# A fixed order for the first four chunks of a gated recurrence, with filler products, and two PSUM banks swapped in the last half

## The chip, the cores and the metric

The kernel runs on one core of a Trainium2 chip. A core has five engines with queues of their own: TensorE (PE, matmuls, with its weight loads as PEld), VectorE (DVE), ScalarE (ACT), GpSimd (POOL) and SyncE (SP, which here issues nearly all transfers). The metric is device time of the whole program in microseconds. The kernel before took 556.48 us, the median of three runs (555.96 to 556.78).

## The reference

Two blocks stand one behind the other. The first is a gated recurrence over 4 batches, 8 heads, 768 positions and a head dimension of 48:

```python
for t in range(S):
    state = alpha[:, :, t, :, None] * state + np.einsum('bhd,bhe->bhde', k[:, :, t], v[:, :, t])
    y[:, :, t] = np.einsum('bhd,bhde->bhe', q[:, :, t], state)
```

Its result, with the heads side by side, is x with 3072 rows and 384 columns. The second block is `h = x @ w_in` (384 x 2048), `g = h * sigmoid(h)`, and `g @ w_out` (2048 x 384). The weights come as 64-bit floats and are turned into 32-bit ones on the chip.

## The kernel before

The recurrence is worked in 24 chunks: 128 positions of one batch, all eight heads in four pairs. Chunk n belongs to batch n mod 4. The first eight chunks take the path that this change touches.

For one chunk, `products(n)` (L710) transposes alpha, k and q on TensorE, four 128x128 transposes each. ScalarE copies the transposed alpha to SBUF (L731). VectorE runs a scan backwards over it (L734), takes the smallest products (L737), multiplies k (L745, tile `kp`), and then, in `quotient`, takes a reciprocal (L762), scans forwards (L764) and multiplies q (L770, tile `p`). `scores(n)` multiplies kp by qp on TensorE, 16 small matmuls into two PSUM tiles; ScalarE copies each to `g` (L812) and GpSimd sets what lies in the future to zero (L813); then kp is transposed and copied to `kn` (L832). `values(n)` multiplies v by g into x (`xt`, copied at L863), and `states(n)` makes the new state from kn and v (L882).

The dense layer is a list of pieces, each 12 or more matmuls long, that `go_on` runs one at a time. The first 16 are `enter_plain` (from L911): 12 matmuls of 128x256 from xt and w_in into one of three PSUM banks, then a Silu on ScalarE (L923). The first needs the x of chunks 0 and 1 and the first three converted pieces of w_in; pieces three and four need six, and so on to twelve. The conversion of one piece is in `weights` (from L614): a transfer of 512 KB of 64-bit words (`bits`, four buffers, issued by SP at L519 in `fetch`), a rounding copy on ScalarE (L629, tile `up`) and three VectorE instructions (L645 to L647). The next rounding copy and the next transfer are issued within the conversion.

The main loop goes over steps. Step s runs scores of chunk s - 1, products of chunk s, values and states of chunk s - 1, and after each of its four slots `fill` (L1184) gives conversions and dense pieces by a due time: up to slot 10 the first three conversions, later pieces, with conversions before each. Through the first steps a planner in the compiler then orders the instructions of each engine by its own costs, and may move any that is not pinned. `keep_in_program_order` pins an instruction behind the one traced before it on its engine. TensorE is pinned only late (`late`, from the end of step 7 at the earliest); in these steps only the rounding copies and the first VectorE instruction of each conversion are.

PSUM has eight banks: three for the recurrence (`ps_a`), three for dense pieces in (`ps_m`), two for dense pieces out (`ps_o`). In the first chunks the transposed k and q use `ps_o` or `ps_m` banks. `leave` (L1035) multiplies g by w_out for half a group: seven pieces, with two accumulators `a` and `b` from `new(i)`, which takes output bank i. The last product of a half is in bank 0, and the half after it starts in bank 0 too. Between halves other work usually lies; at the very end two halves of the last group follow each other directly.

Of the kernel before, what the change touches and what calls it, by code (L numbers as in the profile page):

```python
# [355 lines left out]
def quotients(  # L356
# [23 lines left out]

    def in_order(ins):

        return tc.keep_in_program_order(ins) if late else ins

    class pe:
        @staticmethod
# [49 lines left out]
        return ps_a.tile([128, 512], F32, name="ps_a").rearrange("p (j c) -> p j c", c=n)  # L436


    table = fix.tile([128, 1], F32, name="table")
    dve.memset(table, 0.0)  # L440
    act.activation(table, table, AF.Silu)
    ident = consts.tile([128, 128], F32, name="ident")
    make_identity(nc, ident)

# [21 lines left out]
    def load(n, names="akq"):  # L466
        if n == NT:
            return
        c = ctxs.setdefault(n, dict(zip(("ci", "b"), divmod(n, B))))
        b, rows = c["b"], slice(c["ci"] * C, c["ci"] * C + C)  # L470
        for name, src in (("a", alpha), ("k", k), ("q", q)):
            if name not in names:
                continue
            x = src[b, :, rows, :]
            if n < NA:
                c[name] = nat[name][n % NIN]
                nc.sync.dma_start(c[name][:, :, 0:D], x.transpose([1, 0, 2]))
                continue

            c[name] = late["quads"][name]
            for u in range(2):
                for i in range(2):
                    r = 64 * u + 32 * i
                    nc.sync.dma_start(
                        c[name][r : r + 32, 32 * (1 - i) :][:, 0 : 4 * NP * D].rearrange(
                            "p (g c) -> p g c", g=NP),
                        x[u::2].rearrange("h (b j) d -> b h (j d)", j=4))

    NV = 2
# [4 lines left out]
    def load_v(n):  # L496
        c = ctxs.setdefault(n, dict(zip(("ci", "b"), divmod(n, B))))
        x = v[c["b"], :, c["ci"] * C : c["ci"] * C + C, :].transpose([1, 0, 2])
        t = c["v"] = vns[n % NV]
        if n < NA:  # L500
            nc.sync.dma_start(t[:, :, 0:D], x)
            return
        nc.sync.dma_start(t[:, 0 : H // 2, 0:D], x[:, 0 : H // 2])
        for e in range(2):
            nc.sync.dma_start(t[CH * e : CH * e + CH, H // 2 :, 0:D], x[CH - CH * e : C - CH * e, H // 2 :])
# [7 lines left out]
    def fetch():  # L513

        if wide and sources:
            src = sources.pop(0)
            n = src.shape[1]
            bits = raw.tile([128, 512, 2], I32, name="bits")[:, 0:n, :]
            nc.sync.dma_start(bits.rearrange("p n w -> p (n w)"), src.bitcast(I32))  # L519
            coming.append(bits)  # L520

    load(0)
# [91 lines left out]
    def weights(which):  # L614

        pieces = [
            (w_in[:, t, c : c + 512], moe_w_in[t * 128 : t * 128 + 128, c : c + 512])  # L620
            for t, c in pieces_in
        ] if which == 0 else [
            (w_out[:, f, :], moe_w_out[f * 128 : f * 128 + 128, :]) for f in range(NFT)]
        def rounding(bits):
            n = bits.shape[1]
            up = upp.tile([128, 512], I32, name="up")[:, 0:n]

            tc.keep_in_program_order(
                act.activation(up, bits.bitcast(U32)[:, :, 0], AF.Copy, scale=2.0**-29))  # L629
            return up  # L630

        ahead = []
        for i, (dst, src) in enumerate(pieces):
            if not wide:
                act.dma_start(dst, src)
                yield
                continue
            assert which == 0 or conv_done[0] == n_conv[0]
            bits = coming.pop(0)
            up = ahead.pop() if ahead else rounding(bits)  # L640
            if which == i == 0:
                yield
            hi, w = bits[:, :, 1], dst.bitcast(I32)
            tc.keep_in_program_order(
                dve.tensor_scalar(w, hi, 3, 0x3FFFFFFF, ALU.logical_shift_left, ALU.bitwise_and))  # L645
            dve.scalar_tensor_tensor(w, hi, -(1 << 30), w, ALU.bitwise_and, ALU.bitwise_or)
            dve.tensor_tensor(w, w, up, ALU.add)  # L647
            if i + 1 < len(pieces):
                ahead.append(rounding(coming[0]))
            fetch()  # L650
            yield
# [55 lines left out]
        x = x[:, 32:].rearrange("p (g j d) -> p g j d", j=4, d=D)  # L707
        dve.transpose(to.rearrange("p g (b j) -> p g j b", j=4), x[:, :, :, 0:32])

    def products(n):  # L710

        c = ctxs[n]
        sg = seg[0 if late else n % 2]
        ps = {}

        for name in ("a", "k", "q"):
            if n >= NA:
                if name == "a":
                    turned(c[name], tokens(sg))
                    load(n + 1, "a")  # L720
                continue
            if n < GB and name != "a":

                at = "kq".index(name)
                ps[name] = (bank(at) if n == 1 else out_bank(at, 512)).rearrange("p (j c) -> p j c", c=C)
            else:
                ps[name] = ps_attn()
            for j in range(NP):
                pe.transpose(ps[name][:, j, :], c[name][:, 2 * j : 2 * j + 2, :], ident)
            if name == "a":  # L730
                act.copy(tokens(sg), ps[name])  # L731
        end = NP * W
        u = upool.tile([128, end + 1], F32, name="u")
        dve.tensor_tensor_scan(u[:, end - 1 :: -1], sg[:, end:0:-1], one[:, end:0:-1],  # L734
                               0.0, ALU.mult, ALU.add)

        dve.tensor_single_scalar(least[:, n, :], u[:, 0:end:W], 2.0**-64, ALU.max)  # L737
        kp = c["kp"] = turns(kps, n) if n < NA else kps[0]
        ut = tokens(u)
        if n >= NA:  # L740
# [1 line left out]
            turned(c["k"], ps["k"])  # L742
            load(n + 1, "k")
        if n < NA:
            dve.tensor_tensor(kp, ps["k"], ut, ALU.mult)  # L745
            quotient(n, sg, ps["q"])
            return
        j = NP // 2
# [5 lines left out]
    def quotient(n, sg=None, q=None):  # L754
# [4 lines left out]
                return  # L759
            sg = c.pop("sg")  # L760
        end, iv = NP * W, inv
        dve.reciprocal(iv[:, 0:end:W], least[:, n, :])  # L762
        p = turns(qps if n < NA else [qps[0], late["p"]], n)
        dve.tensor_tensor_scan(p[:, 0:end], sg[:, 0:end], iv[:, 0:end], 0.0, ALU.mult, ALU.add)  # L764
# [5 lines left out]
        dve.tensor_tensor(qp, q, qp, ALU.mult)  # L770

    def flip(n):

# [18 lines left out]
    def scores(n):  # L792
# [6 lines left out]
        for j in (0, 2, 1, 3):  # L799
            for e in range(2 if n >= NA else 1):  # L800
                for u in range(2):
# [5 lines left out]
        g = decayed.rearrange("p (u j c) -> p u j c", u=2, j=NP)  # L807
        swapped = decayed.rearrange("p (o u j c) -> p o u j c", o=2, u=2, j=NP // 2)
        c["g"] = (lambda u, j: g[:, u, j, :]) if n < NA else (
            lambda u, j: swapped[:, j // 2, u, j % 2, :])  # L810
        for u in range(2 if n < NA else 0):
            act.copy(g[:, u], ps[u])  # L812
# [14 lines left out]
        if n < NA and ci < NCH - 1:  # L827
            ps_k = ps_attn()
            for j in range(NP):
                pe.transpose(ps_k[:, j, :], c["kp"][:, j, :], ident)  # L830
            c["kn"] = work.tile([128, NP, C], F32, name="kn")
            act.copy(c["kn"], ps_k)  # L832
        if ci > 0:
            s = st[b].rearrange("p j u e -> p j (u e)")
            for j in range(NP):
# [3 lines left out]

    def values(n):

# [18 lines left out]
        act.copy(xts[half][:, :, e * C : (e + 1) * C], py[:, 0:NKT])  # L863
    def states(n):
        c = ctxs.pop(n)
        ci, b, vn = c["ci"], c["b"], c["v"]
        if ci < NCH - 1:
# [8 lines left out]
            for u in range(2):  # L876
                r = slice(64 * u, 64 * u + D)
                s, x = st[b][r, :, u, :], ps[r, :, 0:D]
                if ci > 0:
                    dve.tensor_tensor(s, x, s, ALU.add)  # L880
                else:
                    act.copy(s, x)  # L882

    def block_x(grp, at):

# [25 lines left out]
    def enter_plain(grp, h, pair):  # L911
# [4 lines left out]
        for f in range(8 * pair, 8 * pair + 8, 2):  # L916
# [6 lines left out]
            act.activation(gts[grp, h, pair][:, i : i + 2, q % 2, :], ps, AF.Silu)  # L923
# [111 lines left out]
    def leave(grp, h):  # L1035
# [30 lines left out]
                sums_w(2 * grp + h - 1, 4 * next(steps) + 4)  # L1066

        def new(i):
            return out_bank(i, HO)

        a, b = new(0), new(1)
        product(a, 0, 0, b11, True)
# [111 lines left out]
    def fill(step, slot):  # L1184

        at = step * SLOTS + slot
        if at < marks[0]:
            if at == SLOTS:
                next(conv[0])
            elif step >= 1:  # L1190
                convert(0, (at - SLOTS) * 3 // (marks[0] - SLOTS) + 1)
            return
        i = next(i for i, m in enumerate(marks[1:]) if at < m)
        a, b = [work_at[n] for n in ([0] + phases)[i : i + 2]]
        due = a + (b - a) * (at - marks[i] + 1) / (marks[i + 1] - marks[i])
# [4 lines left out]
            convert(1, 3 * (done - 6) // 2)  # L1200
            go_on()

    for step in range(STEPS):
        if step == 1:
            load(NIN)
        stages = [[(scores, 1)], [(products, 0)], [(values, 1)], [(states, 1)]]
        if step == 1:

            stages = stages[1::-1] + stages[2:]
        elif 5 <= step < NA:  # L1210
# [105 lines left out]
```

## Time and profile before

| what | us |
| --- | --- |
| median of three runs | 556.48 |
| profiled execution | 557.21 |
| its span, first to last instruction | 555.4 |
| TensorE busy | 540.8 (97%) |
| VectorE busy | 446.1 (80%) |
| ScalarE busy | 208.5 (38%) |
| first transfer of alpha landed, first transpose | 4.1, 4.2 |
| first dense piece starts | 24.23 |
| last matmul ends | 550.4 |

A busy TensorE isn't TensorE at its peak: matmuls overlap, and a slow clock counts as busy. What tells more is the spacing of the starts of successive matmuls. For the 128x256 matmuls of the dense layer it is 216 ns, for the 128x192 ones 163 ns, for a transpose 213 ns at the start of the program and 109 ns later.

### The profile page before, as it was taken

The numbers are of one execution on the slowest core, as the hardware profiler recorded it, in microseconds if no ns is written. First come the engines' busy times: TensorE is split into PE (matmuls) and PEld (weight loads), VectorE is DVE, ScalarE is ACT, GpSimd is POOL, SyncE is SP. The second block draws the span as 40 slices with busy tenths as digits, with TensorE's granted clock in tenths as the row PEclk, the third lists the DMA queues.
The fourth block names the chain that finished last, engine by engine and source line by source line (L and its number), as shares of the span: only waits on it lengthen the run. The fifth ranks groups of instructions, "written<-read, shape, count | busy, mean of one in ns | idle before, by whom it ended". The sixth has DMA issues, their size and how long they took to land. (4 is left out here: it accounts for less than half of the span.)

```text
span 555.4 us, 12641 instructions
## 1 busy us (share of the span) xinstructions
PE 540.8 (97%) x5026; PEld 490.1 (88%) x5026; DVE 446.1 (80%) x801; ACT 208.5 (38%) x466; POOL 76.8 (14%) x146
## 2 busy tenths in 40 slices
PE   6999999999999999999999999999999999999996
PEld 4788887998899899899999999988998999999996
DVE  5897888983999899997998986998884796945431
ACT  2556644223333243353253353343263341332100
POOL 3110100222211212021011021021121000001000
PEclk9999999999999999999999999999999999999999
DMA  9999861254454524345445654707642135500000
GB/s 217 248 252 207 235 192 24 63 157 109 117 144 128 149 70 131 99 125 167 137 109 142 186 142 114 198 22 181 175 133 90 54 90 174 170 9 24 10 27 26
DMA packets 99217, 70.09 MB, mean 126 GB/s; under 512 B 56272, under 2 KB 88656, under 8 KB 99152
## 3 DMA queue, kind: packets, MB, share of 16 engines
q1 hardware_dynamic: 97232, 65.30, 45.0%
q0 software_dynamic: 1920, 3.93, 2.0%
q8 instruction: 40, 0.66, 0.5%
q14 instruction: 25, 0.20, 0.1%
HBM read 61.34 MB, written 7.86 MB: 125 GB/s over the span
## 5 line engine op out<-in xcount | busy, mean ns | idle before, releaser
L388 PE MATMUL ps_o<-w_out,g 128*128 128x192 f32 x768 | 133.8, 328 | 0.7 <-DVE o L1056 0.7
L388 PEld LDWEIGHTS ps_o<-w_out,g 128*128 128x128 f32 x768 | 125.7, 190 | 3.5 <-DVE o L1056 1.2
L388 PE MATMUL ps_m<-xt,w_in 128*128 128x256 f32 x480 | 113.2, 382 | 1.5 <-ACT xt L863 1.1
L388 PEld LDWEIGHTS ps_m<-xt,w_in 128*128 128x128 f32 x480 | 89.2, 190 | 14.4 <-ACT xt L863 1.6
L388 PE MATMUL ps_o<-wt,g 128*128 128x192 f32 x576 | 99.7, 326 | 0.0
L388 PEld LDWEIGHTS ps_o<-wt,g 128*128 128x128 f32 x576 | 95.1, 190 | 1.5
L388 PE MATMUL ps_m<-xc,w_in 128*128 128x256 f32 x288 | 70.7, 382 | 0.0
L388 PEld LDWEIGHTS ps_m<-xc,w_in 128*128 128x128 f32 x288 | 53.7, 190 | 6.9 <-DVE g L958 0.2
L955 ACT ACTIVATE g<-g 128x1024 f32<-128x1024 f32 x32 | 33.1, 1056 | 61.3 <-DVE g L958 61.2
L1047 DVE TENSOR_TENSOR g<-g 128x512 f32<-128x512 f32 x72 | 49.9, 706 | 7.6 <-PE ps_o L388 7.6
L825 POOL TENSOR_SCALAR_AFFINE_SELECT g<-g 64x256 f32<-64x256 f32 x64 | 34.9, 546 | 124.1 <-ACT g L818 105.4
L1059 POOL DMA_DIRECT2D out_dram<-o x40 | 22.0, 551 | 216.3 <-DVE o L1056 111.1
L388 PE MATMUL ps_m<-xc,wx 128*128 128x256 f32 x192 | 50.1, 383 | 1.0 <-DVE xc L586 1.0
L950 ACT COPY g<-ps_m 128x512 f32<-128x512 f32 x64 | 36.5, 588 | 37.1 <-PE ps_m L388 36.9
L388 PEld LDWEIGHTS ps_m<-xc,wx 128*128 128x128 f32 x192 | 35.2, 190 | 5.2 <-ACT u L1078 1.2
L958 DVE TENSOR_TENSOR g<-ps_m,g 128x512 f32<-128x512 f32 x56 | 37.1, 683 | 3.2 <-PE ps_m L388 2.7
L734 DVE TENSOR_TENSOR_SCAN u<-al,one 128x516 f32<-128x516 f32 x24 | 30.1, 1254 | 11.8 <-ACT al L731 11.5
L923 ACT ACTIVATE g<-ps_m 128x512 f32<-128x512 f32 x32 | 19.1, 597 | 40.7 <-PE ps_m L388 40.4
L950 ACT COPY part<-ps_m 128x512 f32<-128x512 f32 x32 | 18.9, 590 | 38.1 <-PE ps_m L388 24.0
L697 DVE TENSOR_REDUCE seen<-bits 128x1 f32<-128x512 int32 (+1 forms) x33 | 26.3, 821 | 6.1 <-DMA bits<-in_moe_w_in_dram 6.1
L764 DVE TENSOR_TENSOR_SCAN p<-al,inv 128x516 f32<-128x516 f32 x24 | 29.9, 1247 | 1.0 <-PE ps_a L388 0.4
L388 PE MATMUL ps_a<-g,vn 128*32 128x128 f32 x768 | 28.0, 282 | 0.5 <-POOL g L813 0.3
(129 smaller groups left out, 630.2 us busy)
## 6 DMA issues: line engine op xcount, KB each, us to landing
bits<-in_moe_w_in_dram SPq DMA_DIRECT2D x24, 512.0 KB, 4.7
bits<-in_moe_w_out_dram SPq DMA_DIRECT2D x16, 384.0 KB, 3.7
at<-in_alpha_dram SPq DMA_DIRECT2D x64, 96.0 KB, 2.6
kt<-in_k_dram SPq DMA_DIRECT2D x64, 96.0 KB, 2.6
qt<-in_q_dram SPq DMA_DIRECT2D x64, 96.0 KB, 2.6
bits<-in_alpha_dram SPq DMA_DIRECT2D x9, 512.0 KB, 4.1
out_dram<-o POOLq DMA_DIRECT2D x40, 96.0 KB, 2.3
flips<-turn SPq DMA_DIRECT2D x12, 256.0 KB, 2.4
```

What stands on the lines that cost most here:

```text
L388: in_order(nc.tensor.matmul(*args, **kw))
L697: dve.tensor_reduce(seen[kind][which][:, i : i + 1], x, axis=AX, op=op, apply_absolute_value=True))
L734: dve.tensor_tensor_scan(u[:, end - 1 :: -1], sg[:, end:0:-1], one[:, end:0:-1], 0.0, ALU.mult, ALU.add)
L764: dve.tensor_tensor_scan(p[:, 0:end], sg[:, 0:end], iv[:, 0:end], 0.0, ALU.mult, ALU.add)
L825: gps.affine_select(x, x, pattern=[[0, NP], [1, CH]], compare_op=ALU.is_ge, fill=0.0, base=0, channel_multiplier=-1)
L923: act.activation(gts[grp, h, pair][:, i : i + 2, q % 2, :], ps, AF.Silu)
L950: act.copy(to, ps)
L955: act.activation(x, x, AF.Silu)
L958: dve.tensor_tensor(to, a, b, op)
L1047: dve.tensor_tensor(cells(grp, h, pair, *to), cells(grp, h, pair, *x), cells(grp, h, pair, *y), ALU.subtract)
L1059: (gps if grp < NG - 1 else nc.sync).dma_start(out[r : r + C, c * HO : (c + 1) * HO], o)
```

## The change

A function `start` replaces the first four steps of the loop. It calls the stages of chunks 0 to 2, the products of chunk 3, all twelve conversions of w_in and seven dense pieces one by one, and while it runs (`stated[0]`) every TensorE instruction is pinned to the order in which it is called, and so are the transfers, the copies on ScalarE and the VectorE instructions that the diff wraps in `settled`. The loop goes on at step 4, without these pins, and the branch of `fill` for the first ten slots is gone. To make the order possible, `products` is split so that its transposes (`bring`) can be called alone, and `scores` so that the transposes of kp (`back`) can come later. Chunk 1 has its own g and kn in a tile `room` from the dense layer's g buffers, so that its scores needn't wait for the values of chunk 0.

`idle(n)` multiplies the identity by itself n times into a PSUM bank that nobody reads. It is called six times ahead of everything, in pairs ahead of five of the first six groups of transposes, and eight times between the kp transposes of chunk 0 and the scores of chunk 1.

In `leave`, the second half of the last group takes the two output banks the other way round.

```diff
     def in_order(ins):
-        return tc.keep_in_program_order(ins) if late else ins
+        return tc.keep_in_program_order(ins) if late or stated[0] else ins
+    stated = [True]
+    def settled(ins):
+        return tc.keep_in_program_order(ins) if stated[0] else ins
...
+    spin = banks[2].tile([128, 512], F32, name="ps_m")
+    def idle(n):
+        for _ in range(n):
+            pe.matmul(spin[:, 0:C], lhsT=ident, rhs=ident, start=True, stop=True)
...
     make_identity(nc, ident)
+    idle(6)
...
+            if n == 0 or n == 1 and name != "q":
+                idle(2)
             for j in range(NP):
                 pe.transpose(ps[name][:, j, :], c[name][:, 2 * j : 2 * j + 2, :], ident)
...
+        if n == 1:
+            room = gpool.tile([128, 4, 2, TB], F32, name="g").rearrange("p a b n -> p (a b n)")
+            c["room"] = room[:, 2 * NP * C :]
+        g = (room[:, 0 : 2 * NP * C] if n == 1 else decayed).rearrange(
+            "p (u j c) -> p u j c", u=2, j=NP)
...
+        if n != 1:
+            back(n)
...
         def new(i):
-            return out_bank(i, HO)
+            return out_bank(i ^ 1 if grp == NG - 1 and h == 1 else i, HO)
...
+    def start():
+        nonlocal bridged
+        w = lambda upto: convert(0, upto)
+        products(0)
+        products(1)
+        load(NIN)
+        next(conv[0])
+        scores(0)
+        w(1)
+        idle(8)
+        scores(1)
+        values(0)
+        back(1)
+        w(2)
+        states(0)
+        values(1)
+        bridged = 2
+        load_v(NV)
+        w(3)
+        states(1)
+        load_v(NV + 1)
+        w(4)
+        bring(2, "a")
+        w(5)
+        go_on()
+        bring(2, "kq")
+        w(6)
+        load(NIN + 1)
+        products(2)
+        go_on()
+        w(7)
+        go_on()
+        scores(2)
+        w(8)
+        go_on()
+        w(9)
+        values(2)
+        states(2)
+        load_v(2 + NV)
+        load(NIN + 2)
+        w(10)
+        bring(3, "a")
+        w(11)
+        bring(3, "kq")
+        go_on()
+        w(12)
+        products(3)
+        load(NIN + 3)
+        go_on()
+        go_on()
+        stated.pop()
+        stated.append(False)
+    start()
+    for step in range(4, STEPS):
```

More of the change, by code (lines that the diff above doesn't have):

```diff
@@ L476, in load @@
                 c[name] = nat[name][n % NIN]
-                nc.sync.dma_start(c[name][:, :, 0:D], x.transpose([1, 0, 2]))
+                settled(nc.sync.dma_start(c[name][:, :, 0:D], x.transpose([1, 0, 2])))
                 continue
@@ L500, in load_v @@
         if n < NA:
-            nc.sync.dma_start(t[:, :, 0:D], x)
+            settled(nc.sync.dma_start(t[:, :, 0:D], x))
             return
@@ L518, in fetch @@
             bits = raw.tile([128, 512, 2], I32, name="bits")[:, 0:n, :]
-            nc.sync.dma_start(bits.rearrange("p n w -> p (n w)"), src.bitcast(I32))
+            settled(nc.sync.dma_start(bits.rearrange("p n w -> p (n w)"), src.bitcast(I32)))
             coming.append(bits)
@@ L645, in weights @@
                 dve.tensor_scalar(w, hi, 3, 0x3FFFFFFF, ALU.logical_shift_left, ALU.bitwise_and))
-            dve.scalar_tensor_tensor(w, hi, -(1 << 30), w, ALU.bitwise_and, ALU.bitwise_or)
-            dve.tensor_tensor(w, w, up, ALU.add)
+            settled(
+                dve.scalar_tensor_tensor(w, hi, -(1 << 30), w, ALU.bitwise_and, ALU.bitwise_or))
+            settled(dve.tensor_tensor(w, w, up, ALU.add))
             if i + 1 < len(pieces):
@@ L708, in turned, with bring @@
         dve.transpose(to.rearrange("p g (b j) -> p g j b", j=4), x[:, :, :, 0:32])
-    def products(n):
+    def bring(n, names="akq"):
         c = ctxs[n]
         sg = seg[0 if late else n % 2]
-        ps = {}
-        for name in ("a", "k", "q"):
+        ps = c.setdefault("ps", {})
+        for name in names:
             if n >= NA:
@@ L730, in products @@
             if name == "a":
-                act.copy(tokens(sg), ps[name])
+                settled(act.copy(tokens(sg), ps[name]))
+    def products(n):
+        if "ps" not in ctxs[n]:
+            bring(n)
+        c = ctxs[n]
+        sg = seg[0 if late else n % 2]
+        ps = c.pop("ps")
         end = NP * W
         u = upool.tile([128, end + 1], F32, name="u")
-        dve.tensor_tensor_scan(u[:, end - 1 :: -1], sg[:, end:0:-1], one[:, end:0:-1],
-                               0.0, ALU.mult, ALU.add)
-        dve.tensor_single_scalar(least[:, n, :], u[:, 0:end:W], 2.0**-64, ALU.max)
+        settled(dve.tensor_tensor_scan(u[:, end - 1 :: -1], sg[:, end:0:-1], one[:, end:0:-1],
+                                       0.0, ALU.mult, ALU.add))
+        settled(dve.tensor_single_scalar(least[:, n, :], u[:, 0:end:W], 2.0**-64, ALU.max))
         kp = c["kp"] = turns(kps, n) if n < NA else kps[0]
@@ L744, in products @@
         if n < NA:
-            dve.tensor_tensor(kp, ps["k"], ut, ALU.mult)
+            settled(dve.tensor_tensor(kp, ps["k"], ut, ALU.mult))
             quotient(n, sg, ps["q"])
@@ L761, in quotient @@
         end, iv = NP * W, inv
-        dve.reciprocal(iv[:, 0:end:W], least[:, n, :])
+        settled(dve.reciprocal(iv[:, 0:end:W], least[:, n, :]))
         p = turns(qps if n < NA else [qps[0], late["p"]], n)
-        dve.tensor_tensor_scan(p[:, 0:end], sg[:, 0:end], iv[:, 0:end], 0.0, ALU.mult, ALU.add)
+        settled(dve.tensor_tensor_scan(
+            p[:, 0:end], sg[:, 0:end], iv[:, 0:end], 0.0, ALU.mult, ALU.add))
         qp = c["qp"] = tokens(p)
@@ L769, in quotient @@
             load(n + 1, "q")
-        dve.tensor_tensor(qp, q, qp, ALU.mult)
+        settled(dve.tensor_tensor(qp, q, qp, ALU.mult))
     def flip(n):
@@ L806, in scores @@
                               start=True, stop=True)
-        g = decayed.rearrange("p (u j c) -> p u j c", u=2, j=NP)
+        if n == 1:
[3 more added lines that the diff above has]
+            "p (u j c) -> p u j c", u=2, j=NP)
         swapped = decayed.rearrange("p (o u j c) -> p o u j c", o=2, u=2, j=NP // 2)
@@ L811, in scores @@
         for u in range(2 if n < NA else 0):
-            act.copy(g[:, u], ps[u])
+            settled(act.copy(g[:, u], ps[u]))
             gps.affine_select(g[:, u], g[:, u], pattern=[[0, NP], [1, C]], compare_op=ALU.is_ge,
@@ L826, in scores @@
                                       compare_op=ALU.is_ge, fill=0.0, base=0, channel_multiplier=-1)
[L827 to L832, printed above, removed]
+        if n != 1:
+            back(n)
         if ci > 0:
@@ L838, in scores, with back @@
                     tc.keep_in_program_order(mul)
+    def back(n):
+        c = ctxs[n]
+        if n >= NA or c["ci"] == NCH - 1:
+            return
+        ps_k = ps_attn()
+        for j in range(NP):
+            pe.transpose(ps_k[:, j, :], c["kp"][:, j, :], ident)
+        c["kn"] = c.pop("room")[:, 0 : NP * C].rearrange("p (j c) -> p j c", j=NP) if (
+            "room" in c) else work.tile([128, NP, C], F32, name="kn")
+        settled(act.copy(c["kn"], ps_k))
     def values(n):
@@ L862, in values @@
             xts[half] = xtp.tile([128, NKT, TB], F32, name="xt")
-        act.copy(xts[half][:, :, e * C : (e + 1) * C], py[:, 0:NKT])
+        settled(act.copy(xts[half][:, :, e * C : (e + 1) * C], py[:, 0:NKT]))
     def states(n):
@@ L881, in states @@
                 else:
-                    act.copy(s, x)
+                    settled(act.copy(s, x))
     def block_x(grp, at):
@@ L922, in enter_plain @@
             q, i = divmod(f, 4)
-            act.activation(gts[grp, h, pair][:, i : i + 2, q % 2, :], ps, AF.Silu)
+            settled(act.activation(gts[grp, h, pair][:, i : i + 2, q % 2, :], ps, AF.Silu))
             if grp == 1 and pair == h == 0:
@@ L1186, in fill @@
         at = step * SLOTS + slot
[L1187 to L1192, printed above, removed]
         i = next(i for i, m in enumerate(marks[1:]) if at < m)
@@ L1201, in fill @@
             go_on()
-    for step in range(STEPS):
-        if step == 1:
-            load(NIN)
+    def start():
[52 more added lines that the diff above has]
+    for step in range(4, STEPS):
         stages = [[(scores, 1)], [(products, 0)], [(values, 1)], [(states, 1)]]
-        if step == 1:
-            stages = stages[1::-1] + stages[2:]
-        elif 5 <= step < NA:
+        if 5 <= step < NA:
             stages = stages[0:2] + [stages[2] + stages[3], []]
```

## The prediction

> **What bounds the kernel now.** I read the page's engine shares first, then the windows view cut where the traffic on TensorE changes, then the timelines of TensorE and VectorE over the first 50 us, and last the gaps between matmul starts.
>
> ```profile
> PE 540.8 (97%) x5026; PEld 490.1 (88%) x5026; DVE 446.1 (80%) x801; ACT 208.5 (38%) x466; POOL 76.8 (14%) x146
> ...
> 0.00:24.20 24.20, 18.79 (x202) 14.01 (x202) 15.94 (x29) 10.21 (x20) 7.50 (x25) 1.00 1.10 236
> 24.20:49.50 25.30, 25.27 (x202) 20.87 (x203) 22.07 (x37) 13.74 (x26) 3.10 (x4) 1.00 0.86 235
> 49.50:520.00 470.50, 466.81 (x4442) 425.90 (x4441) 398.45 (x717) 183.28 (x417) 66.21 (x117) 1.00 0.45 122
> ```
>
> The second to fourth lines give a stretch and its length, then busy time of PE, weight loads, DVE, ACT and POOL. From 24.2 us on, TensorE is never idle for long. The end is therefore set by when a given amount of PE work is finished, and a gain in the head is kept unless a later wait eats it. Over the first 24.2 us things are different: the same length of time holds 202 small matmuls and not one piece of the dense layer.
>
> ```profile
> 13.04 1.11 PE L392 MATMUL ps_a<-ident,kp 128*128 128x128 f32 x4
> 17.75 1.66 PE L388 MATMUL ps_a<-p,kp 48*128 48x128 f32 x16
> 19.34 0.66 PE L392 MATMUL ps_a<-ident,kp 128*128 128x128 f32 x4
> 24.23 2.86 PE L388 MATMUL ps_m<-xt,w_in 128*128 128x256 f32 x12 [0.26 <-ACT xt L863]
> 27.22 2.86 PE L388 MATMUL ps_m<-xt,w_in 128*128 128x256 f32 x12
> 30.01 1.16 PE L388 MATMUL ps_a<-p,kp 48*128 48x128 f32 x16
> 31.59 2.76 PE L388 MATMUL ps_m<-xt,w_in 128*128 128x256 f32 x12
> ...
> 531.95 2.87 PE L388 MATMUL ps_o<-w_out,g 128*128 128x192 f32 x16 [0.51 <-DVE o L1056]
> ```
>
> Columns: start, length, instruction. The same four transposes take 1.11 us at 13.04 and 0.66 at 19.34; a score stage (16 matmuls) takes 2.08 at 11.03 and 1.16 at 30.01. TensorE ran at half speed until the middle of the stage at 17.75; the clock column above says 1.00 for it because the trace's first clock record is the release itself, at 18.8. The first two dense pieces (12 matmuls each) start at 24.23 and 27.22. The last row is the only sizeable wait of the tail.
>
> ```profile
> 6.09 1.23 DVE L734 TENSOR_TENSOR_SCAN u<-al,one 128x516 f32<-128x516 f32 x1 [4.70 <-ACT al L731]
> 10.19 1.22 DVE L734 TENSOR_TENSOR_SCAN u<-al,one 128x516 f32<-128x516 f32 x1
> 14.28 0.43 DVE L645 TENSOR_SCALAR w_in<-bits 128x512 int32<-128x512 int32 x1
> 14.75 1.00 DVE L646 SCALAR_TENSOR_TENSOR w_in<-bits,w_in 128x512 int32<-128x512 int32 x1
> 16.50 0.42 DVE L645 TENSOR_SCALAR w_in<-bits 128x512 int32<-128x512 int32 x1
> 22.14 1.23 DVE L734 TENSOR_TENSOR_SCAN u<-al,one 128x516 f32<-128x516 f32 x1 [1.77 <-ACT al L731]
> 26.24 0.42 DVE L645 TENSOR_SCALAR w_in<-bits 128x512 int32<-128x512 int32 x1
> 28.02 0.42 DVE L645 TENSOR_SCALAR w_in<-bits 128x512 int32<-128x512 int32 x1
> ```
>
> These rows give the prices of VectorE: one chunk's `products` takes 4.10 us (6.09 to 10.19, 10.19 to 14.28, 22.14 to 26.24); one converted piece of w_in takes 1.8 to 1.9 (26.24 to 28.02; I use 1.89), or 2.2 with a POOL select beside it (14.28 to 16.50).
>
> [...] from 4.2 to 14.2 us TensorE had almost no gap, mostly transposes, and stayed slow; it was released at 18.8, after 3 to 4 us of values, states and scores.[...]
>
> **The change, part by part.** *The bank swap.* Before the last half, PE waits for the last store's sum to leave bank 0: the matmul at 531.95 starts 0.67 us later than its usual spacing of 163 ns. With the banks swapped the half starts in the other bank, whose last reader (the u3 sum) ran at 528.88. The second product then takes bank 0, free at 531.90, and isn't due before 534. Gain 0.67.
>
> *Idle products.* Six, five pairs and eight: 24 products at the transposes' price, 213 ns slow, 109 fast: 5.1 us at most. The first eight lie between the identity (ready at 1.53) and the first input (4.08), so the first scan stays at 6.09. The pairs push the second alpha transpose from 7.71 to about 8.3 and its copy's end to about 10.1, still before VectorE is free at 10.19. The third k and q transposes come later, about 11.4, and the first scores start at 11.4 instead of 11.03. The eight run at 14.2 to 15.9 if PE is still slow, and put the second scores at 15.9, where 14.4 would be possible; before, they were at 17.75. Thus the fillers cost PE time only where other things are late anyway. Without that cover they would cost 2.6 to 5.1. [...] they may release the clock earlier; the trace has none of these, so anything from 9 to 19 us can be its time. I take 16.
>
> *Two scores first, on PE.* Second scores 15.9 to 17.1, values(0) 1.0, kp transposes 0.5, states(0) 0.5, then values(1) after POOL's second select at 19.1 (two copies at 0.59, selects at 0.65 behind them), states(1), chunk 2's alpha at 20.7. First dense piece at 21.2, not 24.23. Its w_in (three pieces) is ready at 20.3.
>
> *VectorE's order.* Now three more conversions stand ahead of chunk 2's products. 6.09 + 2 x 4.10 = 14.28; pieces 1 to 3 end at 20.3 as before; the fourth at about 22.4. The fifth needs a transfer issued at 16.33 that landed at 22.79 in this trace, the sixth one that landed at 24.19; SP issues both behind the same transfers as before. So 22.8 + 2 x 1.89 = 26.6, products(2) to 30.75, scores(2) at 30.85, against 30.01 before. PE fills that time with pieces one to three (21.2 to 29.9, chunk 2's k and q between) and then has a hole of up to 1 us. This is why an earlier clock is worth little: scores(2) stands behind VectorE in either case. ACT too is kept in order: each rounding copy stands ahead of later copies, and the fifth (needs the 22.79 landing) ahead of chunk 2's alpha copy, done at about 24.1, 2.5 before it is wanted.
>
> *From there on.* Before, from scores(2) at 30.01 to chunk 4's alpha transposes at 49.52: 19.51 us, with five dense pieces. After, with four pieces left (7 minus 3) at 2.7: 16.8, so 30.85 + 16.8 = 47.7: a gain of 1.9. But VectorE has six conversions (6 x 1.89 + 0.5 for the select beside them = 11.9) and products(3) (4.1): 30.75 + 16.0 = 46.75, and scores(3) could otherwise start at 45.95. That is another hole of 0.9, partly filled if the planner takes a transpose of chunk 4 first. The head's gain is thus 1.0 to 1.9; I take 1.4.
>
> *Moved transfers.* Chunk 3's a, k and q now go to SP's queue behind v of chunks 2 and 3 and four w_in pieces; issue about 26 to 29, landing by 34, wanted at 36.6. Chunk 4's are issued at about 37 for 47. Moving g and kn of chunk 1 into a spare g buffer costs nothing: that tile is free until the second pair of dense pieces.
>
> Sum: 1.4 + 0.67 = 2.1. The profiled execution took 557.21 (span 555.4, the rest around it), so 555.1 in its terms; the median of the runs is 556.48, 0.7 below it, which gives **554.4**.
>
> **Rivals.** A change within 0.2% (1.1 us) is about what a measurement of this kernel can't tell from none.
> *Tail alone.* VectorE's chain slips by another 1 to 2 us (a 0.67 us `g` addition was run at 40.8 amid products(3), and roundings may come late on ACT). For it: 22.07 of 25.3 us were busy already. Then the head gives nothing: 556.48 - 0.67 = 555.8.
> *More than that.* The gap before the fifth conversion closes (0.6), the planner fills the second hole, and a small wait such as the 0.47 at 55.2 goes too: 1.9 + 0.6 + 0.5 + 0.67 = 3.7, so 552.8. More is excluded by VectorE's sum above.
> *Slower.* The fixed order has no way round a late transfer. If the sixth w_in piece lands after 24.7, scores(2) and all dense work behind it move by the same. At 26.8 the gain is gone; at 29 it is 2.2 worse: 558.7. Against it: nothing ahead of that transfer on SP's queue is changed.
> *No real change of order*, because the planner keeps its own: the pins cover every PE instruction of the stretch, so I give that nothing.
>
> **How the numbers follow.** Forecast 0.55 (553.3 to 555.3), more than that 0.14, tail alone 0.18, slower 0.13. Range 553.0 to 556.1: it leaves out the slower case and a little of the largest gains, and takes in the clock, which moves the holes but not scores(2). Forecast and larger gain make faster 0.69; tail alone makes same 0.18; slower 0.13.
>
> **What would show it.** First dense piece at 20 to 21.5; three of them before scores(2); scores(2) at 30 to 31.5 straight after products(2), with a PE gap before it; seventh piece over by 46; no wait at 530 for the store's sum. The forecast is wrong if scores(2) starts after 32, if the first scan leaves 6.1, or if later waits on PE grow by over 1 us.

## The result and the profile after

The changed kernel took 557.79 us (median of 18 runs, 556.95 to 559.10) beside 556.70 for the kernel before (18 runs, 555.53 to 557.23): a ratio of 1.0026, 95% interval 1.0019 to 1.0033. It is slower by a quarter of a per cent; the forecast was 554.4 and faster. The profiled execution took 557.68, its span is 555.9, against 557.21 and 555.4.

The engine shares of the page and the windows view of the changed kernel, cut as before (stretch, length, busy time of PE, weight loads, DVE, ACT and POOL):

```profile
PE 540.4 (97%) x5074; PEld 493.8 (89%) x5074; DVE 446.2 (80%) x801; ACT 208.9 (38%) x466; POOL 76.8 (14%) x146
...
0.00:24.20 24.20, 20.61 (x256) 18.85 (x257) 16.63 (x30) 12.00 (x23) 8.76 (x25) 1.00 1.10 247
24.20:49.50 25.30, 22.29 (x193) 19.22 (x192) 22.18 (x36) 11.36 (x21) 1.80 (x2) 1.00 0.93 243
49.50:520.00 470.50, 466.63 (x4443) 425.19 (x4440) 397.15 (x716) 184.22 (x419) 66.25 (x119) 1.00 0.46 121
```

In the first stretch TensorE does more than before, fillers and a dense piece among it. In the second it is busy for 22.29 us where it was for 25.27: it now waits 3 us there, and VectorE is as full as it was (22.18 against 22.07). The body is unchanged. So the stretch from 24 to 50 us, which TensorE limited before, now has waits of TensorE in it; the experiments test whether VectorE is what it waits for.

TensorE's timeline after:

```profile
1.58 3.79 PE L394 MATMUL ps_m<-ident 128*128 128x128 f32 x16 [1.58 <-POOL ident masks.py:199]
5.16 1.06 PE L398 MATMUL ps_a<-ident,an 128*128 128x128 f32 x4
...
15.76 1.16 PE L394 MATMUL ps_a<-p,kp 48*128 48x128 f32 x16 [0.97 <-DVE p L796]
...
21.70 2.75 PE L394 MATMUL ps_m<-xt,w_in 128*128 128x256 f32 x12
...
25.17 5.35 PE L394 MATMUL ps_m<-xt,w_in 128*128 128x256 f32 x24
31.64 1.23 PE L394 MATMUL ps_a<-p,kp 48*128 48x128 f32 x16 [1.13 <-DVE p L796]
...
38.70 7.94 PE L394 MATMUL ps_m<-xt,w_in 128*128 128x256 f32 x36
48.52 1.25 PE L394 MATMUL ps_a<-p,kp 48*128 48x128 f32 x16 [1.89 <-DVE p L796]
...
50.38 0.65 PE L398 MATMUL ps_a<-ident,an 128*128 128x128 f32 x4
...
532.51 2.76 PE L394 MATMUL ps_o<-w_out,g 128*128 128x192 f32 x16
```

The first row is the first eight identity products: 16 records, two for each, where a transpose has one. They end after the first alpha has landed (4.14), and its transposes begin at 5.16, not 4.2. The second scores (15.76) come 2 us earlier and the first dense piece 2.5 us earlier than before. Then TensorE waits 1.13 us ahead of chunk 2's scores and 1.89 ahead of chunk 3's, both times for the `p` that VectorE makes. The last row is the output half that had waited for its bank; it now has no wait. The row at 50.38 is chunk 4's alpha; the same row of the kernel before:

```profile
49.52 0.60 PE L392 MATMUL ps_a<-ident,an 128*128 128x128 f32 x4
```

The head thus ends 0.86 us later than it did.

VectorE's timeline after:

```profile
7.01 1.23 DVE L759 TENSOR_TENSOR_SCAN u<-al,one 128x516 f32<-128x516 f32 x1 [5.62 <-ACT al L748]
...
11.11 1.22 DVE L759 TENSOR_TENSOR_SCAN u<-al,one 128x516 f32<-128x516 f32 x1
...
13.25 1.56 DVE L789 TENSOR_TENSOR_SCAN p<-al,inv 128x516 f32<-128x516 f32 x1
...
15.52 0.42 DVE L659 TENSOR_SCALAR w_in<-bits 128x512 int32<-128x512 int32 x1
...
27.41 1.23 DVE L759 TENSOR_TENSOR_SCAN u<-al,one 128x516 f32<-128x516 f32 x1
...
31.50 0.42 DVE L659 TENSOR_SCALAR w_in<-bits 128x512 int32<-128x512 int32 x1
...
37.54 0.69 DVE L662 CUSTOM_DVE_ANT_0 w_in<-w_in,up 128x1024 uint16<-128x1024 uint16 x1 [0.59 <-ACT up L643]
...
39.21 0.68 DVE L1072 TENSOR_TENSOR g<-g 128x512 f32<-128x512 f32 x1
...
44.20 1.23 DVE L759 TENSOR_TENSOR_SCAN u<-al,one 128x516 f32<-128x516 f32 x1
...
47.68 0.69 DVE L796 TENSOR_TENSOR p<-ps_o,p 128x512 f32<-128x512 f32 x1
```

From 7.01 on VectorE works almost without a pause: two chunks' products, six conversions (15.52 to 27.41), chunk 2's products, six conversions (31.50 to 44.20), chunk 3's products. The last row makes the `p` that chunk 3's scores wait for; it ends at 48.37, and they start at 48.52. Nearly every start here is the sum of what stands ahead of it.

The same matmuls, compared from profile to profile, start 1.02 us later at 55 to 80 us, 1.29 later from 86 on (a small wait at 85.5), 1.23 at 512, and 0.45 behind the bank swap. The swap therefore gained 0.78, and the head, planned to gain, lost 1.0.

### The profile page after: what moved, and what is told of

Its sections match the earlier page's. It is cut to its first block, busy times and chain, and to the rows that moved or that the text cites. A ratio compares the mean times of both kernels' runs of the same rounds, so it can differ in the third digit from the quotient of the medians.

```text
span 555.9 us, 12731 instructions
## 1 busy us (share of the span) xinstructions
PE 540.4 (97%) x5074; PEld 493.8 (89%) x5074; DVE 446.2 (80%) x801; ACT 208.9 (38%) x466; POOL 76.8 (14%) x146
## 5 line engine op out<-in xcount | busy, mean ns | idle before, releaser
L759 DVE TENSOR_TENSOR_SCAN u<-al,one 128x516 f32<-128x516 f32 x24 | 29.6, 1234 | 11.2 <-ACT al L748 10.9
L394 PEld LDWEIGHTS ps_a<-p,kp 48*64 48x64 f32 (+1 forms) x640 | 20.0, 144 | 11.9 <-issue 7.2
```

Of the source, the lines that this page charges most:

```text
L394: in_order(nc.tensor.matmul(*args, **kw))
L759: settled(dve.tensor_tensor_scan(u[:, end - 1 :: -1], sg[:, end:0:-1], one[:, end:0:-1], 0.0, ALU.mult, ALU.add))
```

## The experiments

Theory A: VectorE's sum of scans and conversions sets the scores of chunks 2 and 3, so the order on TensorE gains nothing, and whatever lengthens that sum costs. Rivals: B, that the fillers themselves cost the time; C, that the place of the conversions is at fault, and that products ahead of them would do; D, that the clock is what matters. The expectations use the letters less strictly; where that matters, it is said. The ratios are to the kernel before, run beside each, with 95% intervals.

### The swap alone, in the kernel before

```diff
-            return out_bank(i, HO)
+            return out_bank(i ^ 1 if grp == NG - 1 and h == 1 else i, HO)
```

> The kernel before with the two output banks of the last half swapped and nothing else. Theory A: PE's wait before the last half goes, 0.7 to 0.8 us shorter than the kernel before, with nothing changed ahead of 530 us. If the swap only moves the wait to the half's second product, no difference.

Measured: 555.38 beside 555.81, ratio 0.9989 (0.9982 to 0.9996). TensorE's timeline near the end, the half that had waited:

```profile
530.93 2.76 PE L388 MATMUL ps_o<-w_out,g 128*128 128x192 f32 x16
```

No wait is left. This part of the change works as forecast. On its own it is faster than the kernel before, and of the kernels here that compute the whole reference it has the lowest ratio.

### Without the first six products

```diff
     make_identity(nc, ident)
-    idle(6)
```

> The changed kernel without its first six identity products. Theory A (VectorE's chain is what counts: the sixteen half-products ahead of chunk 0's first transposes run to 5.2 us and put the first scan at 7.01 instead of 6.09): with two fillers left there, the first scan is back at 6.1, every later link of VectorE's chain comes 0.9 earlier, scores(2) at about 30.75, scores(3) at about 47.6, and the whole is 0.9 us shorter than the changed kernel. Theory B (the six release the clock early, and that is worth more than they cost): the clock is released after 11, the second scores start after 16.5, and the time is that of the changed kernel or longer.

Measured: 557.27 beside 555.81, ratio 1.0018 (1.0012 to 1.0025). TensorE's timeline, then the windows view of 45 to 55 us (the third number from the end is the clock):

```profile
47.28 1.25 PE L394 MATMUL ps_a<-p,kp 48*128 48x128 f32 x16 [1.89 <-DVE p L795]
48.46 0.77 PE L398 MATMUL ps_a<-ident,kp 128*128 128x128 f32 x4
49.14 1.12 PE L398 MATMUL ps_a<-ident,an 128*128 128x128 f32 x4
...
45.00:55.00 10.00, 8.11 (x58) 6.72 (x60) 5.91 (x9) 5.01 (x12) 1.22 (x2) 0.83 0.92 191
```

The first scan moved from 7.01 to 5.94, and chunk 3's scores from 48.52 to 47.28: the delay by the first eight products runs right through VectorE's chain to the scores, as A says. But little of it arrived in the median. The hole ahead of the scores is still 1.89, and behind it the clock fell to half: the four transposes at 49.14 take 1.12 us instead of 0.65. It stayed half from 48.87 to 52.28, and the matmul that starts at 59.21 in the changed kernel starts 0.16 later here, so that in this profile the whole lead of 1.24 is lost. Of 21 runs, 14 had a mean clock of 0.996 or less, and all of these had the longer spans (555.3 to 555.9 against 554.3 to 555.0; the medians differ by 1.05). The mean clock of a run is only a rough sign of such a stretch, since it takes in the last microseconds, after the last matmul, too (0.65 from 552 to 556 in the profile of the changed kernel, with TensorE idle). Taken group by group, the median spans are 0.7 to 1.25 us shorter than those of the changed kernel, as A has it; but more of the runs are in the group of the lower clock, 14 of 21 where the changed kernel has 15 of 34 in its two sets of runs. These ran on different chips, and why the share is larger is not shown.

### No fillers at all

```diff
-        for _ in range(n):
+        for _ in range(0):
```

> The changed kernel with no identity products at all. Theory A: first scan at 6.1, the clock released only at 15 to 19, but the slow stages before that only use up holes; scores(2) and scores(3) stand where VectorE lets them, as without the first six alone, so 0.9 us shorter than the changed kernel. Theory B: without fillers TensorE is slow until about 18 and the first dense piece starts after 23, the time is over 0.5 us longer than the changed kernel.

Measured: 557.08 beside 555.81, ratio 1.0019 (1.0012 to 1.0027), as without the first six. TensorE's timeline:

```profile
9.88 0.84 PE L398 MATMUL ps_m<-ident,qn 128*128 128x128 f32 x4
10.65 1.16 PE L394 MATMUL ps_a<-p,kp 48*128 48x128 f32 x16
11.74 0.66 PE L398 MATMUL ps_a<-ident,kp 128*128 128x128 f32 x4
14.46 1.16 PE L394 MATMUL ps_a<-p,kp 48*128 48x128 f32 x16 [2.07 <-DVE p L796]
```

The clock was released at 10.3 with only transposes ahead of it, amid the group at 9.88. Chunk 2's scores came at 30.95 and chunk 3's at 47.83, so B explains at most the first scan's delay: with no fillers the order is still slower than before. The expectation had the clock released at 15 to 19 and 0.9 us gained on the changed kernel; the release came much earlier, and the ratios differ by 0.05 to 0.07%, 0.3 to 0.4 us. That the fillers fill waits is true (2.07 ahead of the second scores is empty here), but these waits don't set chunk 3's scores.

### Chunk 3's products ahead of the last three conversions

```diff
-        w(10)
         bring(3, "a")
-        w(11)
         bring(3, "kq")
         go_on()
-        w(12)
         products(3)
+        w(10)
+        w(11)
+        w(12)
         load(NIN + 3)
         go_on()
-        go_on()
```

The seventh piece is left to the loop. In this expectation the letters stand the other way round: what it calls A is C here, and its rival C is A.

> The changed kernel with products(3) ahead of the last three conversions, and with its seventh dense piece left to the loop. Theory A (the 1.9 us hole before scores(3) comes from three conversions, 5.7 us and more, put ahead of products(3) on VectorE): scores(3) starts at 44 to 44.5 right behind the sixth dense piece, instead of 48.52, and 1.4 to 2 us of the whole are saved. Rival C (VectorE's sum is what counts, whatever its order): the seventh piece then waits for the twelfth conversion, done at about 48.5 either way, a hole of over 1 us opens before or in it, and less than 0.7 us is saved.

Measured: 558.67 beside 555.81, ratio 1.0051 (1.0031 to 1.0071). TensorE's timeline:

```profile
43.98 1.16 PE L394 MATMUL ps_a<-p,kp 48*128 48x128 f32 x16
...
46.74 0.70 PE L394 MATMUL ps_m<-xt,w_in 128*128 128x256 f32 x2 [0.58 <-DVE w_in L662]
49.41 1.99 PE L394 MATMUL ps_m<-xt,w_in 128*128 128x256 f32 x8 [1.98 <-DVE w_in L662]
```

The scores come 4.5 us earlier and without a hole, and the seventh dense piece waits for the conversions instead, 0.58 and 1.98. C falls: the sum on VectorE is the same, and what is put behind is waited for.

### The changed kernel again

No edit.

> The changed kernel unaltered, to have it on the same chip and in the same rounds as the others. 0.2 to 0.5% above the kernel before by both theories; its runs fall in two groups, those with a mean clock of 0.996 or less (half speed for some 3.4 us after the hole before scores(3)) about 1 us longer.

Measured: 557.29 beside 556.04, ratio 1.0024 (1.0015 to 1.0033). TensorE's timeline:

```profile
48.47 1.29 PE L394 MATMUL ps_a<-p,kp 48*128 48x128 f32 x16 [1.89 <-DVE p L796]
49.69 0.66 PE L398 MATMUL ps_a<-ident,kp 128*128 128x128 f32 x4
50.33 1.10 PE L398 MATMUL ps_a<-ident,an 128*128 128x128 f32 x4
```

In this profile the clock fell at 50.38 for 3.4 us, behind the same hole; in the one shown above it did not. Of the 16 runs 7 had a mean clock of 0.996 or less (spans 555.7 to 557.3); the others took 555.2 to 555.6. So the hole ahead of chunk 3's scores has two prices: its own length always (1.89 us in both profiles), and, by this sign, a slow stretch in about half of the executions.

### The hole ahead of chunk 3's scores filled

To the kernel without the first six, seven identity products in a fresh bank are added:

```diff
         go_on()
         go_on()
+        rest = banks[1].tile([128, 512], F32, name="ps_m")
+        for _ in range(7):
+            pe.matmul(rest[:, 0:C], lhsT=ident, rhs=ident, start=True, stop=True)
         stated.pop()
```

> The changed kernel without its first six identity products and with seven put into the hole before scores(3) (14 half-products of 112 ns, 1.6 of its 1.9 us). Theory E (TensorE's hole of 1.9 us before scores(3) lets the clock fall to half for 3.4 us in most runs, 1 us each): scores(3) starts where it did, no run with a mean clock of 0.996 or less, median 0.6 to 0.9 us below the kernel without the first six alone. Otherwise the same time as that.

Measured: 556.01 beside 556.04, ratio 1.0000 (0.9992 to 1.0008). TensorE's timeline:

```profile
45.83 1.72 PE L394 MATMUL ps_m<-ident 128*128 128x128 f32 x14
47.79 1.16 PE L394 MATMUL ps_a<-p,kp 48*128 48x128 f32 x16 [0.24 <-DVE p L795]
...
49.68 0.66 PE L398 MATMUL ps_a<-ident,an 128*128 128x128 f32 x4
```

The transposes behind it stay fast, and all 14 runs had a clock of 0.997 or more. Against the changed kernel on the same chip that is 1.28 us, but this kernel also lacks the first six products; against the kernel that lacks only these it is 0.18% of the ratio, 1.0 us, measured on another chip. So D (E in the expectation) holds for this one place. It makes the change even with the kernel before, and no better, although the swap is in it; the order by itself still loses what the swap gains.

### Five fillers, in the kernel before, without and with the swap

```diff
+    spin = banks[2].tile([128, 512], F32, name="ps_m")
+    for _ in range(5):
+        tc.keep_in_program_order(
+            nc.tensor.matmul(spin[:, 0:C], lhsT=ident, rhs=ident, start=True, stop=True))
```

D stands here for this: a release earlier than the 18.8 us in the forecast's profile makes the head of the kernel before shorter.

> The kernel before with five identity products ahead of its first transposes (ten half-products of 213 ns from 1.58 us, over by 3.9) and nothing else. Theory D ([...] the wait before the third chunk's products shrinks): the clock is released before 11, the first dense piece starts before 23, chunk 2's first scan at 20.4 to 21, spans of 553.3 to 554.0 and a median 0.2 to 0.6 us below the kernel before, with fewer long runs. If the release is without effect on the end, no difference.

> The kernel before with the bank swap and with five identity products ahead of its first transposes. By theory D and the swap alone (0.4 to 0.8 us): 0.7 to 1.3 us below the kernel before, the fastest of all here.

Measured: 560.78 (ratio 1.0076, 1.0058 to 1.0094) and, with the swap, 559.65 (1.0062, 1.0044 to 1.0080), both beside 556.04. TensorE's timeline of the first, then its window from 10 to 20 us:

```profile
12.72 2.08 PE L388 MATMUL ps_a<-p,kp 48*128 48x128 f32 x16 [2.09 <-DVE p L774]
...
19.96 2.09 PE L388 MATMUL ps_a<-p,kp 48*128 48x128 f32 x16
...
10.00:20.00 10.00, 7.08 (x90) 5.73 (x90) 9.48 (x16) 3.44 (x7) 1.92 (x2) 0.61 1.19 306
```

The clock was released at 5.4, and then lost at 12.21 while TensorE waited for its first scores (2.09): it stayed half until 22.45, for 10 us, through two score stages of 2.1 each. The planner had also put chunk 1's first scan ahead of chunk 0's `p`, so that the wait is partly of its making; how much of the 3.55 us lost by 55 us is the order and how much the clock these two runs do not divide. In the second of them, with the swap, the same hole (2.11) is followed by half clock from 14.15 to 24.39 (mean clock of the execution 0.991, of the first 0.990), and 1.88 us are lost by 55 us. Both were forecast to be faster. They show that fillers which release the clock early needn't make this head shorter; what an early release alone is worth they do not tell.

### The kernel before again

No edit.

> The kernel before, unaltered, for a second trace of it. Theory D (the profile that the forecast was made from had a late release of the clock, at 18.8 us, and its 557.21 us was long for it): in most executions the release comes before 13 us, chunk 2's first scan follows the third conversion without the 1.77 us wait, the first dense piece starts at 22 to 23.5 and the span is 553.3 to 554.3. If the release comes at 18 again, the span is over 554.3.

Measured: 556.40 beside 556.12, ratio 0.9998 (0.9988 to 1.0007). Its profile had the release at 18.8 again, with a span of 555.2. Over the 151 runs of it in these experiments its spans lay from 553.3 to 555.9, half of them at 554.3 or less, and so the profile of before that the forecast was made on (555.4) is one of its longer executions. The expectation's claim that most executions have an early release is not shown: of the profiles with this head, this one, the one of the forecast and that of the swap alone have it at 18.5 to 18.8, and one, shown next, earlier.

### VectorE's work made shorter, in both kernels

The third instruction of conversions seven to twelve (0.69 us each), which adds the rounding, is left out; six pieces of w_in are then cut off and not rounded. It is done in the changed kernel and in the one before:

```diff
-            settled(dve.tensor_tensor(w, w, up, ALU.add))
+            if which or i < 6:
+                settled(dve.tensor_tensor(w, w, up, ALU.add))
```

> The changed kernel without the last of the three VectorE instructions (the addition of the rounding) in conversions 7 to 12, so that w_in is cut off there, not rounded: 6 x 0.83 = 5.0 us less on VectorE between products(2) and products(3), everything else in place. Theory A (VectorE's sum sets scores(3)): scores(3) starts at 45.9 to 46.7, right behind the seventh dense piece; the hole of 1.9 us and the fall of the clock after it are gone; 1.9 us shorter than the changed kernel, and 2.4 in the median. If the hole comes from something else (a transfer, ACT, the order on PE), scores(3) stays after 47.5.

> The kernel before with the same six instructions left out (w_in's conversions 7 to 12 cut off, not rounded). Theory A: TensorE doesn't wait for VectorE there, so the time is within 0.15% of the kernel before. If VectorE's work in the head is a bound in the kernel before as well, it is over 0.5 us shorter.

Measured: changed 555.03 beside 556.12, ratio 0.9975 (0.9964 to 0.9986); before 556.20, ratio 0.9997 (0.9989 to 1.0005). TensorE's timeline of the changed kernel with this omission:

```profile
38.70 7.94 PE L394 MATMUL ps_m<-xt,w_in 128*128 128x256 f32 x36
46.57 1.16 PE L394 MATMUL ps_a<-p,kp 48*128 48x128 f32 x16
```

The scores stand right behind the three pieces, no hole and no slow stretch follow, and half a per cent is gained against the changed kernel (0.9975 against 1.0024 and 1.0026, or 2.7 us). The same omission gives the kernel before nothing. Of the four theories only A foretells both: VectorE is what chunk 3's scores wait for in the new head, and it is not seen to bind the old one.

The profile of the lighter kernel before shows a second thing. TensorE's timeline:

```profile
11.06 1.23 PE L388 MATMUL ps_a<-p,kp 48*128 48x128 f32 x16
...
22.89 2.86 PE L388 MATMUL ps_m<-xt,w_in 128*128 128x256 f32 x12 [0.26 <-ACT xt L864]
...
28.66 1.16 PE L388 MATMUL ps_a<-p,kp 48*128 48x128 f32 x16
```

Here the clock was released at 11.2, and the first scores take 1.23 instead of 2.08. The first dense piece then starts at 22.89, not 24.23, and chunk 2's scores at 28.66, not 30.01, though none of the lightened conversions lies ahead of either. In such an execution the head of the kernel before is 1.4 us shorter than in the profile that the forecast used, and the lead stays: 1.45 us at 51 us and 1.30 at 492. At 51 us the lighter changed kernel, which has no hole ahead of chunk 3's scores, leads the same profile by only 0.91. So even without that hole the new head isn't shown to be shorter than the old one with an early release. (In the median the lighter changed kernel is 0.22% below the lighter kernel before, and the swap alone gives 0.11.)

### Scans ahead of conversions, in all the stretch

Without the first six; chunk 2's products come after three conversions, chunk 3's after six; chunk 3's scores, values and states are taken into the fixed stretch; and step 4 of the loop has only `products(4)`. The core of it:

```diff
-        w(4)
         bring(2, "a")
-        w(5)
...
+        w(4)
         scores(2)
-        w(8)
-        go_on()
-        w(9)
+        w(5)
+        bring(3)
+        w(6)
...
+        w(7)
+        scores(3)
+        w(8)
+        values(3)
+        states(3)
```

What this expectation calls A is again nearer to C, a better order, and its last sentence is A.

> The changed kernel without its first six products and with another fixed order: products(2) behind three conversions instead of six and products(3) behind six instead of twelve, chunk 3's values and states inside the fixed stretch ahead of the pieces that need the later conversions. Theory A (order the chain so that TensorE always has attention work while VectorE converts): scores(2) before 27.5, scores(3) before 37.5, no TensorE hole over 1 us after 21 us, and 1 to 3 us below the kernel before. If VectorE's sum up to the twelfth conversion is what counts, the holes come back before dense pieces three, five or seven, and it is no faster than the kernel before.

Measured: 556.96 beside 556.12, ratio 1.0012 (1.0004 to 1.0020). TensorE's timeline:

```profile
37.84 1.16 PE L394 MATMUL ps_a<-p,kp 48*128 48x128 f32 x16
...
40.86 0.41 PE L394 MATMUL ps_a<-g,vn 128*32 128x128 f32 x4 [1.27 <-POOL g L843]
41.90 0.96 PE L394 MATMUL ps_a<-g,vn 128*32 128x128 f32 x26 [0.62 <-POOL g L843]
```

Chunk 3's scores come at 37.84 and wait for nothing, but values behind them wait for GpSimd's selects (1.27 and 0.62) with no dense piece between; the clock was half from 43.03 to 46.44, and later VectorE itself waited for ScalarE's rounding copies (1.71 and 0.84). The order was to be 1 to 3 us faster than the kernel before and is slower than it; against the kernel without the first six (1.0018) the intervals overlap, so that it isn't shown to be a better order than the change's either.

## Why the prediction was wrong

The forecast was 555.1 in the profile's terms and the profile gave 557.68. Of these 2.6 us the head made 2.4 (a gain of 1.4 forecast, a loss of 1.02 at 55 us), a wait at 85.5 some 0.27, and the swap gave 0.1 back. The step that failed is the head's gain of 1.0 to 1.9: VectorE's sum in it was 1.67 us too short, and the second hole, taken as partly filled, stayed empty.

**The swap: right.** Named 0.67, measured 0.78; alone it is 0.11% in the runs.

**"24 products at the transposes' price ... the first scan stays at 6.09": wrong.** An identity product leaves two records of 213 ns at half clock, where a transpose leaves one; the first eight took from 1.58 to 5.16, not to about 3.3, and the scan began at 7.01. The step had named its cover (the first alpha's landing at 4.08) and did not ask at which price that cover ends. At 16 x 213 ns it is overrun by 1 us; "if the first scan leaves 6.1" was listed as a sign of failure, and it was the first to show.

**VectorE's sum: right as a mechanism, 1.6 us short.** Conversions one to six ended at 27.41 (26.6 named): 0.92 from the first scan and 0.3 from chunk 1's forward scan (1.56 for 1.23 while GpSimd selects), less 0.4 because the fifth piece had not to wait. The second six took 12.70 and not 11.9: 0.46 for a late rounding copy (the 0.59 idle ahead of 37.54, where 0.14 is usual: on ScalarE the copy came right behind a Silu that had waited 1.06 us for the fourth dense piece) and 0.37 for the `g` addition, which now landed amid the tenth. Both had been named as the reasons of the rival "tail alone", and were left out of the sum. So chunk 3's scores started at 48.52 and not at 46.85.

**"Partly filled": wrong.** The working had two holes ahead of scores, up to 1 and 0.9. They came out at 1.13 and 1.89, and nothing filled the second: the stretch is pinned up to there, and the first stage on TensorE behind it is these scores; the planner put nothing ahead of them. From their start to chunk 4's alpha is 1.86, which puts that alpha at 48.7 by the forecast's own 46.85; the 48.1 that it stood for had 0.6 of filling in it. With the 1.67 above this is the whole miss of the head at that alpha (50.38).

**"An earlier clock is worth little": wrong for a loss of it.** The release came at 7.1, and the first dense piece came no earlier than forecast for a release at 16 (21.70, 21.2 named). But the hole of 1.9 led to a slow stretch of 3.4 us in about half of the executions, about 1 us each; filling the hole took about 1.0 us from the median. The profile compared above had no such stretch, so this comes on top in the median. The working had weighed only when the clock is released, not that a hole made by the change can lose it again.

**The baseline: one execution taken for the kernel.** Steps such as "scores(2) 30.85, against 30.01 before" compare with an execution released at 18.8. With a release at 11.2 those scores stand at 28.66, and the first piece at 22.89. Moving the sum to the median by 0.7 treated this as a constant around the program. In part it lay in the head, the place that was to be made shorter, so that some of the gain was already there in some of the executions; how many release early is not known.

**The clock's release.** The 16 of the forecast was an estimate within 9 to 19, and the release came at 7.1. With fillers ahead it came at 5.4 (five in the kernel before) and 7.1 (the changed kernel), without them at 10.3, 11.2 and 18.5 to 18.8; what brings it was not shown. In the profile of before TensorE was busy for 9.29 of the 10 us from 5 to 15, mostly with transposes, and stayed slow, but without fillers in the changed order it was released at 10.3 behind nothing but transposes. The releases at 11.2 and 18.8, in the same head, lie 7.6 us apart; the forecast had one profile of it and gave the release of the kernel before no range.

**Signs and rivals.** The first dense piece at 21.70 and chunk 2's scores at 31.64 were just outside the stretches named, the seventh piece ended at 46.64 and not by 46; three pieces ahead of the scores and no wait at 530 came true. The rival that ended slower named a late transfer. It was not that: the sixth piece landed at 23.61, and the moved transfers of chunks 3 and 4 by 34.55 and 46.23, in time. The wait of 0.47 at 55.2 in the rival "more than that" is 0.27 in TensorE's timeline, and stayed. The mechanism of "tail alone", further along, is what took place: it was given 0.18 and ended at 0 for the head, where the chain can end below it. The small wait at 85.5 goes back to a transfer of w_out, which took 4.12 us where it had taken 3.86: ScalarE's rounding copy waited for it (82.50, against 81.22 before), and the copy of alpha behind that ended at 85.98, 0.09 ahead of the matmuls that had waited (before, at 84.70 and as close ahead of them). The second profile of the changed kernel has no such loss. Left open are the split between the order and the clock in the kernel before with five fillers, and why the same hole is followed by a slow stretch in some executions only.

## What to carry to other kernels

When an order is changed to feed one engine, add up the other engine's queue from its first instruction to the last result that is wanted, with every small instruction in it, and compare that date with the old one; taking work from that queue in both kernels (here six additions) shows which of the two it binds. A filler has to be priced as what it is (here two records of 213 ns at half clock, not one) and ended before the data come, and a hole costs its length (here 1.89 us) and then perhaps the clock (here half for 3.4 us, about 1 us more, in about half of the executions). Look at more than one execution of the kernel before, since the one profiled may hold a delay that others do not have.

## What the runs showed of the hardware

- A 128x128 matmul in 32-bit floats left two records of 213 ns each at half clock (16 records in 3.4 us of starts for eight products, in the changed kernel), a transpose of the same size one.
- TensorE's clock fell to half behind single holes of 1.89 us (without the first six, and in the second profile of the changed kernel), 2.09 and 2.11 (five fillers in the kernel before, without and with the swap), and behind two of 1.27 and 0.62 with 0.4 us of work between them (scans ahead of conversions). It did not in every execution: with no fillers, holes of 2.07 and 2.00, and in the first profile of the changed kernel one of 1.89, left it at full speed (mean clock 0.998 in both).
- Once lost, the clock stayed half for 3.41 us in three profiles (48.87 to 52.28, 50.38 to 53.80, 43.03 to 46.44) and for 10.24, three times as long, in the two kernels with five fillers (12.21 to 22.45, 14.15 to 24.39), although in the first of these TensorE was busy for 7.08 of the 10 us from 10 on, at a mean clock of 0.61.
